# Layer one's first matrix in groups 4 to 7 by seven half-block products instead of eight, for two of the three token blocks

## The chip, the core and the metric

The kernel runs on one core of one Trainium2 chip. The metric is the time of one execution on the device, in microseconds.

## The reference

Attention over 2 x 8 heads with a window and block sums, then two feed-forward layers. The change touches layer one (`_moe_ref`):

```python
# x: 1536 tokens x 512, from the attention
h = x @ w_in                                  # 512 x 2048
x = (h * (1.0 / (1.0 + np.exp(-1.702 * h)))) @ w_out    # 2048 x 512
gate = 1.0 / (1.0 + np.exp(-(x @ w_gate)))    # layer two, 512 x 1536 each
out = (gate * (x @ w_val)) @ w_out2           # 1536 x 512
```

## The kernel before

The tokens are three blocks of 512 (`blk` 0 to 2), held transposed: 128 partitions x 4 chunks of 128 channels x 512 tokens. Every number that TensorE multiplies is split into a high and a low half (`xH`, `xL`; of a weight H and L), and a product of two is three matmuls: low x high, high x low, high x high. A group `g` is 256 columns of the first matrix and the same 256 rows of the second; layer one has 8 groups, layer two 6.

`first` (L368) makes the two 128-column halves of `x @ w_in` for one group and one block: 2 x 12 matmuls of 128x128 by 512 into PSUM banks `ps_h` (`project`, L352), then for each the sigmoid on ScalarE and `gate_by` (L358): the product with the sigmoid on VectorE, its high half (`gh`) on ScalarE, its low half (`gl`) on GpSimd. `second` (L395) multiplies `gh` and `gl` with the second matrix in four m-steps of 6 matmuls (`ps_o`), each added into the SBUF tile `acc` on VectorE (L429). `mm3` (L344) issues the matmuls of both.

Layer two does blocks 0 and 1 of its first matrices in another way, `pair` (L262). A group's two column halves and the two channel halves (LO, HI) make a 2x2 matrix of half blocks, blocks 0 and 1 by channel halves another, and seven products ("1" to "7") of half blocks or of sums of them stand for the eight plain ones. The sums of the weights come from `combine` (L200): high and low half are added again (L205), four sums are built (L214) and split (L219, L220). The sums of the inputs come from `token_sums` (L239). Products share banks x, v and y: product 1 is copied from x into y, 2 adds into x, 6 and 7 and then 4 add into y, 3 into v behind 5; `keep` (L285) copies a bank to SBUF and `total` (L289) adds it to another. Block 2 goes the plain way by half products, `single` (L323).

Weights come as 64-bit words, by 1 MB DMAs on SP's queue (`fetch`, L157), two at a time. `decode` (L91) makes H and L of a matrix with four VectorE instructions of 128x1024 (L102, L105, L107, L112) and two on ScalarE; it is a generator of five parts, and `pull` draws one part between the pieces of the main work. H and L lie in rings of 8, 4 and 2 tiles (`w_slots`, `w_a`, `w_b`, `w_c`), 14 in all; a group's load starts at a fixed step of the main loop.

Groups 0 and 1, blocks 0 and 1, run between the attention's units. Behind the attention (from L746) the steps are (g, blk), each a `first` with the `second` of the step before. `first` has 2 PSUM banks (`ps_h`) and `second` 6 (`ps_o`); in layer two it is the other way round.

The order of SP's instructions is the written one. That of every other engine is chosen when the program is built, by a planner that plays it through with durations of its own: of the instructions that are ready it takes the one written first. `keep_in_program_order` ties an instruction behind the one that was written before it on its engine, in issue order alone. An instruction that writes a tile waits for the last reader of what lay in its place.

Of the kernel before, what the change touches and what calls it, by code (L numbers as in the profile page):

```python
# [28 lines left out]
def attention_moe_moe2_kernel(ctx: ExitStack, tc: tile.TileContext, ins: dict, out: bass.AP):  # L29
# [34 lines left out]
    class Slots:  # L64


        def __init__(self, tag):
            self.tag, self.order, self.i = tag, [], 0

# [14 lines left out]
    w_slots, sg_slots, gh_slots, gl_slots = (Slots(t) for t in ("w", "sg", "gh", "gl"))  # L84
    w_a = pool([w_slots], 8, "w_a")
# [5 lines left out]
    def decode(raw, hi_out, lo_out):  # L91
# [8 lines left out]
        ts = nc.vector.tensor_scalar  # L100

        ts(out=af, in0=head.bitcast(F32), scalar1=F64_MAX, scalar2=-F64_MAX, op0=ALU.min, op1=ALU.max)  # L102
        nc.scalar.activation(af, af, AF.Prelu, scale=REBIAS, alpha=-2.0 ** 32)  # L103
        yield
        ts(out=b, in0=tail, scalar1=29, scalar2=None, op0=ALU.logical_shift_right)  # L105
        yield
# [3 lines left out]
        nc.scalar.copy(hi_out, af)  # L110
        yield
        nc.vector.tensor_tensor(out=lo_out, in0=af, in1=hi_out, op=ALU.subtract)  # L112
        yield
# [18 lines left out]
    groups = [(1, g) for g in range(n1)] + [(2, g) for g in range(n2)]  # L132
    steps = [(1, g, blk) for blk in range(NTB) for g in range(2)]
    steps += [(1, g, blk) for g in range(2, n1 - 2) for blk in range(NTB)]
    steps += [(1, g, blk) for g in (n1 - 2, n1 - 1) for blk in range(2)] + [(1, g, 2) for g in (n1 - 2, n1 - 1)]
# [11 lines left out]
    pieces, weights, raws, ready = [], {}, [], {}  # L147
# [20 lines left out]
    def load(slots, layer, g, i):  # L168
        raw, shape = raws.pop(0)
        hi, lo = (slots.tile(list(shape), F32R, name=f"w{layer}_{g}_{i}{x}") for x in "HL")  # L170
        parts = decode(raw, hi.rearrange("p a n -> p (a n)"), lo.rearrange("p a n -> p (a n)"))
        for step, _ in enumerate(parts):
            if step == 1 and (layer, g) != (1, 0):
                fetch()
            yield
        return hi, lo

    def load_group(layer, g):
        tiles = weights[layer, g] = []
        ready[layer, g] = 0  # L180
        for i in range(len(mats[layer])):
            tiles += yield from load(w_slots, layer, g, i)
            ready[layer, g] += 1
            yield

    class Ring:


        def __init__(self, pool):
            self.pool = pool  # L190

        def tile(self, shape, dtype, name):
            return self.pool.tile(shape, dtype, tag="w", name=name)

# [5 lines left out]
    def combine(g, i):  # L200

        hi, lo = weights[2, g, i]
        flat = "p a n -> p (a n)"
        w, s = (wtmp.tile([P, KC, GF * P], F32, tag=t, name=f"{n}{g}_{i}") for t, n in (("da", "wf"), ("db", "ws")))
        nc.vector.tensor_tensor(out=w.rearrange(flat), in0=hi.rearrange(flat), in1=lo.rearrange(flat), op=ALU.add)  # L205
        yield
        s = s.rearrange("p a (k f) -> p a k f", f=P)
        for n, a, b, op in (
            (0, block(w, 1, 0), block(w, 1, 1), ALU.add),
            (1, s[:, 0], block(w, 0, 0), ALU.subtract),  # L210
            (2, block(w, 0, 0), block(w, 1, 0), ALU.subtract),
            (3, block(w, 0, 1), s[:, 1], ALU.subtract),
        ):
            nc.vector.tensor_tensor(out=s[:, n], in0=a, in1=b, op=op)  # L214
            if n % 2:
                yield
        sh, sl = (Ring(w_b).tile([P, 4, KC // 2, P], F32R, name=f"s{x}{g}_{i}") for x in "HL")
        flat = "p a k f -> p (a k f)"
        nc.scalar.copy(sh.rearrange(flat), s.rearrange(flat))  # L219
        nc.vector.tensor_tensor(out=sl.rearrange(flat), in0=s.rearrange(flat), in1=sh.rearrange(flat), op=ALU.subtract)  # L220
        sums[g, i] = sh, sl
        yield

    sums = {}

    def prepare():

        for g in range(-1, n2):
            for n in ([0, 1] if g < 0 else [0, 2, 1]):
                to = g + (n != 2)  # L230
                if to < n2:
                    weights[2, to, n] = yield from load(Ring(w_c if n == 2 else w_a), 2, to, n)
                    ready[2, to, n] = 1
                    yield
            for n in range(2 * (g + 1 < n2)):
                yield from combine(g + 1, n)
                ready[2, g + 1, "s", n] = 1

    def token_sums():  # L239
# [3 lines left out]
        for name, x, y, to in (  # L243
# [6 lines left out]
            if name == "4":  # L250
                h, l = xH[1][:, LO], xL[1][:, LO]
            else:
                h, l = (tp.tile([P, KC // 2, TB], F32R, tag=f"t{name}{x}", name=f"t{name}{x}") for x in "HL")
# [8 lines left out]
    def pair(g):  # L262


        def sums_of(n, i):
            return tuple(x[:, n] for x in sums[g, i])

        def a(i, r, c):
            return tuple(block(x, r, c) for x in weights[2, g, i])
# [11 lines left out]
        def new(b, i):  # L281
            ps[b, i] = ps_f.tile([P, TB], F32, tag="o", name=f"ps_{b}")
# [10 lines left out]
        def out(i, to, x, own=None):  # L293
            if i:
# [5 lines left out]
        for n in "1256734":  # L300
            for i in range(2):
# [21 lines left out]
    def single(g):  # L323

        for f in range(GF):
            sg = None
            for i in range(2):
                wh, wl = weights[2, g, i]
                ps = ps_f.tile([P, TB], F32, tag="o", name="ps_h" if i == 0 else "ps_v")
# [5 lines left out]
                if i == 0:  # L335
                    sg = sg_slots.tile([P, TB], F32, "sg")
                    nc.scalar.activation(sg, ps, AF.Sigmoid)
                else:
                    gate_by((2, g, 2, f), ps, sg)
# [12 lines left out]
    def project(wh, wl, f, blk, name):  # L352
        ps = ps_h.tile([P, TB], F32, tag="h", name=name)
# [14 lines left out]
    def first(layer, g, blk, batch=False):  # L368
        w = weights[layer, g]
# [25 lines left out]
    def second(layer, g, blk, last, lag=False):  # L395
        wh, wl = weights[layer, g][-2:] if layer == 1 else weights[2, g, 2]
# [7 lines left out]
        for m in range(4):  # L404
            ps = ps_o.tile([P, 512], F32, tag=o_tag, name="ps_o")
# [3 lines left out]
            elif last and blk == NTB - 1 and m == 3:  # L409

                r0 = blk * TB + m * P
                for n0 in range(0, 512, 256):
                    n = slice(n0, n0 + 256)
                    if n0:
                        ps = ps_o.tile([P, 512], F32, tag=o_tag, name="ps_o")
# [24 lines left out]
    ps_o, o_tag = ps_h, "h"  # L440
# [3 lines left out]
    coming = (x for n in range(2) for x in load_group(*groups[n]))  # L444

    def pull(n):
        for _ in range(n):
            if next(coming, True):
                break

    def need(layer, g, n):
        while ready.get((layer, g), 0) < n:
            pull(1)

    with tc.manual_schedule(engines={mybir.EngineType.SP}), ExitStack() as es:
# [236 lines left out]
        def filler():  # L692
            for layer, g, blk in steps[:EARLY]:
                while (blk + 1) * 2 * HP - 1 + LD > now[0]:
                    yield
                need(layer, g, len(mats[layer]) - 1)
                yield from first(layer, g, blk, batch=True)
                need(layer, g, len(mats[layer]))
# [47 lines left out]
    with tc.manual_schedule(engines={mybir.EngineType.SP}):  # L746
        w_b, w_c = pool([w_slots], 4, "w_b"), pool([w_slots], 2, "w_c")
# [4 lines left out]
        ps_o = ctx.enter_context(tc.tile_pool(name="ps_o", bufs=6, space=PSUM, reuse_waits="tile"))  # L752
        o_tag = "o"
        pull(1000)
        coming = load_group(*groups[2])
        pull(1)
        prev, folding = None, iter(())
        for step in steps[EARLY:]:
            layer, g, blk = step
            need(layer, g, len(mats[layer]) - 1)  # L760
            for _ in first(*step):
                pull(1)
                next(folding, None)
            if prev:
                need(*prev[:2], len(mats[prev[0]]))
                for _ in second(*prev, prev[1] == ends[1]):
                    pull(1)
                    next(folding, None)
                if prev == (1, n1 - 1, 1):
                    folding = token_sums()  # L770
            prev = step
            if blk == (NTB - 1 if g < 2 else 0) and (1, g + 1) in groups and (1, g + 1) not in ready:
                pull(1000)
                coming = load_group(1, g + 1)
            elif step == (1, n1 - 1, 0):
                pull(1000)
                coming = prepare()
        ps_f, ps_o, o_tag = ps_o, ps_h, "h"

        def ahead(g):  # L780
            if (2, g, "s", 1) not in ready:
                pull(1)

        for g in range(n2):
            for key in ((2, g, 0), (2, g, 1), (2, g, "s", 0), (2, g, "s", 1)):
                while key not in ready:
                    pull(1)
            for _ in folding:
                pass
            rest = second(*prev, prev[0] == 1)  # L790
            for slot, _ in enumerate(pair(g)):
# [7 lines left out]
            while (2, g, 2) not in ready:  # L799
                pull(1)  # L800
            rest = (x for blk in range(2) for x in second(2, g, blk, g == ends[2]))
# [49 lines left out]
```

## Time and profile before

| | us |
|---|---|
| median of 3 runs | 628.73 |
| lowest, highest | 628.70, 629.77 |
| the profiled execution | 629.99 |
| its span, from the first to the last instruction | 628.1 |
| TensorE, VectorE, ScalarE, GpSimd busy in it | 613.1, 430.8, 282.5, 194.8 |

The granted TensorE clock is 0.997 of full speed over the span. PE is TensorE, DVE is VectorE, ACT is ScalarE, POOL is GpSimd; L349 is line 349. A matmul's record lasts some 390 ns and overlaps the next one's, so TensorE's time is read from the distance between starts. Idle time of an engine that nothing waits for costs nothing.

### The profile page before, as it was taken

To read this page: it belongs to the slowest core of one execution; us is meant where nothing else is said; L and a number is where in the kernel's file an instruction comes from. 1 tells how busy PE (TensorE), PEld (TensorE's weight loads), DVE (VectorE), ACT (ScalarE), POOL (GpSimd) and SP (SyncE) were. 2 spreads that over 40 slices of the span, in tenths; PEclk is the share of its full clock that TensorE was granted. 3 is DMA by queue.
4 is the path that set the end of the run, shared out by engine and by line. 5 is a ranking of instruction groups with operands and counts; after the bars stand their busy time and mean duration, and the time that the engine had idled before them with its cause. 6 is when DMAs were issued, how large, how long until landed. Compare 5 with 4: busy or idle time off the path is not lost.

```text
span 628.1 us, 8342 instructions
## 1 busy us (share of the span) xinstructions
PE 613.1 (98%) x3162; PEld 499.9 (80%) x3162; DVE 430.8 (69%) x628; ACT 282.5 (45%) x560; POOL 194.8 (31%) x164
## 2 busy tenths in 40 slices
PE   7898999999999999999999999999999999999997
PEld 4676787778888888888888887888887888888886
DVE  6699666488976665565379995279499479496524
ACT  4688657546443334232246645444344244333310
POOL 6797676233132313132222030120031120130210
PEclk9899999999999999999999999999999999999999
DMA  9997752044521222100001304012113012100004
GB/s 311 347 328 254 242 126 64 2 134 141 176 86 67 68 67 68 67 2 1 0 13 61 129 0 135 0 68 78 57 67 118 17 67 74 61 1 0 2 33 168
DMA packets 25160, 58.08 MB, mean 92 GB/s; under 512 B 1568, under 2 KB 1824, under 8 KB 25120
## 3 DMA queue, kind: packets, MB, share of 16 engines
q1 hardware_dynamic: 24400, 56.24, 27.6%
q10 hardware_dynamic: 720, 1.31, 0.6%
q8 instruction: 25, 0.41, 0.3%
q14 instruction: 15, 0.12, 0.1%
HBM read 53.08 MB, written 3.15 MB: 90 GB/s over the span
## 4 chain that ended last, share of the span: by engine, by line
PE 86%; DVE 9%; ACT 2%; issue 1%; DMA 1%; SPq 0%; DVEq 0%; ACTq 0%
PE ps_o L349 35%; PE ps_h L349 20%; PE ps_v L124 8%; PE ps_y L124 7%; PE ps_x L124 5%; PE ps_h L124 4%; PE ps_s L559 3%; PE ps_x L611 2%; PE ps_p L592 1%; DVE wf L205 1%; DVE ws L214 1%; DMA vt<-in_vt 1%; ACT e L572 1%; DVE nm L564 1%; DVE sg L364 1%
## 5 line engine op out<-in xcount | busy, mean ns | idle before, releaser
L366 POOL TENSOR_TENSOR gl<-sg,gh 128x512 fp32r<-128x512 f32 x84 | 119.5, 1424 | 393.7 <-ACT gh L365 372.0
L429 DVE TENSOR_TENSOR acc<-ps_o,acc 128x512 f32<-128x512 f32 x143 | 97.2, 686 | 56.9 <-PE ps_o L349 56.8
L365 ACT CAST gh<-sg 128x512 fp32r<-128x512 f32 x84 | 52.0, 620 | 89.8 <-DVE sg L364 79.6
L349 PE MATMUL ps_o<-gh,w_1L 128*128 128x512 f32 x192 | 74.5, 395 | 1.6 <-ACT gh L365 1.5
L349 PE MATMUL ps_h<-xH,w_0L 128*128 128x512 f32 x192 | 75.2, 396 | 0.5 <-DVE acc L429 0.5
L349 PE MATMUL ps_o<-gl,w_1H 128*128 128x512 f32 x192 | 75.4, 393 | 0.0
L349 PE MATMUL ps_h<-xL,w_0H 128*128 128x512 f32 x192 | 75.0, 391 | 0.0
L349 PE MATMUL ps_o<-gh,w_1H 128*128 128x512 f32 x192 | 74.8, 390 | 0.0
L349 PE MATMUL ps_h<-xH,w_0H 128*128 128x512 f32 x192 | 74.8, 390 | 0.0
L364 DVE TENSOR_TENSOR sg<-ps_h,sg 128x512 f32<-128x512 f32 x48 | 32.9, 687 | 44.1 <-ACT sg L373 43.8
L349 PE MATMUL ps_o<-w_2H,gl 128*128 128x512 f32 (+1 forms) x146 | 56.2, 388 | 1.0 <-ACT acc L425 0.6
L349 PE MATMUL ps_o<-w_2H,gh 128*128 128x512 f32 (+1 forms) x146 | 56.4, 386 | 0.0
L349 PE MATMUL ps_o<-w_2L,gh 128*128 128x512 f32 (+1 forms) x146 | 56.4, 386 | 0.0
L373 ACT ACTIVATE sg<-ps_h 128x512 f32<-128x512 f32 x48 | 28.3, 595 | 61.2 <-PE ps_h L349 61.2
L107 DVE SCALAR_TENSOR_TENSOR da<-da,db 128x1024 uint32<-128x1024 uint32 x34 | 43.9, 1290 | 14.4 <-ACT da L103 14.0
L103 ACT ACTIVATE da<-da 128x1024 f32<-128x1024 f32 x34 | 36.1, 1061 | 30.6 <-DVE da L102 28.6
L349 PEld LDWEIGHTS ps_o<-gh,w_1L 128*128 128x128 f32 x192 | 35.9, 188 | 9.3 <-ACT gh L365 2.0
L349 PEld LDWEIGHTS ps_h<-xH,w_0L 128*128 128x128 f32 x192 | 36.0, 188 | 8.2 <-DVE acc L429 0.9
L349 PEld LDWEIGHTS ps_h<-xH,w_0H 128*128 128x128 f32 x192 | 36.0, 188 | 7.6
L349 PEld LDWEIGHTS ps_o<-gh,w_1H 128*128 128x128 f32 x192 | 36.1, 188 | 7.3
L349 PEld LDWEIGHTS ps_o<-gl,w_1H 128*128 128x128 f32 x192 | 36.1, 188 | 7.3 <-POOL gl L366 0.2
L349 PEld LDWEIGHTS ps_h<-xL,w_0H 128*128 128x128 f32 x192 | 36.0, 188 | 7.4
(162 smaller groups left out, 1244.5 us busy)
## 6 DMA issues: line engine op xcount, KB each, us to landing
raw<-in_moe_w_out SPq DMA_DIRECT2D x13, 1024.0 KB, 4.9
raw<-in_moe_w_in SPq DMA_DIRECT2D x8, 1024.0 KB, 7.3
raw<-in_moe_w_gate SPq DMA_DIRECT2D x6, 1024.0 KB, 5.1
raw<-in_moe_w_val SPq DMA_DIRECT2D x6, 1024.0 KB, 5.1
q<-in_q SPq DMA_DIRECT2D x20, 256.0 KB, 7.5
vwin<-in_v SPq DMA_DIRECT2D x6, 768.0 KB, 8.1
k<-in_k SPq DMA_DIRECT2D x8, 400.0 KB, 6.5
out<-acc SPq DMA_DIRECT2D x11, 256.0 KB, 2.0
```

What stands on the lines that cost most here:

```text
L103: nc.scalar.activation(af, af, AF.Prelu, scale=REBIAS, alpha=-2.0 ** 32)
L107: nc.vector.scalar_tensor_tensor(out=a, in0=a, scalar=3, in1=b, op0=ALU.logical_shift_left, op1=ALU.bitwise_or)
L124: nc.tensor.matmul(ps, lhsT=a[x][:, kk, :], rhs=b[y][:, kk, :], start=start and i == 0, stop=i == n - 1, skip_group_check=True,)
L205: nc.vector.tensor_tensor(out=w.rearrange(flat), in0=hi.rearrange(flat), in1=lo.rearrange(flat), op=ALU.add)
L349: nc.tensor.matmul(ps, lhsT=a, rhs=b, start=i == 0, stop=i == n - 1)
L364: nc.vector.tensor_tensor(out=sg, in0=val, in1=sg, op=ALU.mult)
L365: nc.scalar.copy(gh, sg)
L366: nc.gpsimd.tensor_tensor(out=gl, in0=sg, in1=gh, op=ALU.subtract)
L373: nc.scalar.activation(sg, ps, AF.Sigmoid, scale=1.702 if layer == 1 else 1.0)
L429: nc.vector.tensor_tensor(out=a[:, m, :], in0=ps, in1=a[:, m, :], op=ALU.add)
L559: nc.tensor.matmul(ps[:, j, :], lhsT=t[:, j, :], rhs=kt[:, j, :], start=False, stop=j == G - 1)
L611: nc.tensor.matmul(ps[64 * e:64 * e + 64, j, :], lhsT=x[:, h * D:(h + 1) * D], rhs=y[:, j, 64 * e:64 * e + 64], start=n == 0, stop=n == le ...
```

## The change

- In groups 4 to 7 of layer one, blocks 0 and 1 of the first matrix go through `pair(1, g)`, block 2 through `single(1, g)`. Both now take the layer; layer one has one first matrix, the order "1526374", and each finished piece gets its own sigmoid and gate.
- `input_sums` makes the sums of the attention's output in 13 parts: eight parts behind step (2, 0), the rest behind step (3, 1). Its adds on VectorE are kept in program order, the low halves are GpSimd's. Sum "4" overwrites the low channel half of block 1.
- `load` joins `decode` and `combine`, for both layers: the sums are built from the decoded float before it is split, so the add of high and low halves (L205) is gone.
- The rings of weight tiles become 14 named places, 8 and 6: `take` gives the oldest free one, `drop` frees a matrix behind its last use, and the loads run on through all matrices in one order, whenever two tiles are free.
- PSUM behind the attention: 4 banks for the first steps, 4 for the second steps; in layer two 6 and 2 as before.
- The second steps of groups 4 to 7 run inside the pairs and singles, block 1 before block 0. `pair(1, 7)` runs straight behind `pair(1, 6)`; `single(1, 6)` follows it.

The core of the diff:

```diff
+    def take(shape, name, key):
+        p, tag = w_free.pop(0)
+        w_held.setdefault(key, []).append((p, tag))
+        return p.tile(shape, F32R, tag=tag, name=name)
+    def drop(*key):
+        w_free.extend(w_held.pop(key))
...
+    def load(layer, g, i, early):
+        while len(w_free) < 2:
+            yield
...
+        nc.vector.tensor_tensor(out=lo.rearrange(flat), in0=af, in1=hi.rearrange(flat), op=ALU.subtract)
+        weights[layer, g, i] = hi, lo
+        yield
+        if layer == 1 and (g < PAIRED or i == 1) or layer == 2 and i == 2:
+            yield
+            return
+        w = af.rearrange("p (a n) -> p a n", n=shape[2])
+        s = wtmp.tile([P, 4, KC // 2, P], F32, tag="db", name=f"ws{layer}_{g}_{i}")
...
-        nc.vector.tensor_tensor(out=w.rearrange(flat), in0=hi.rearrange(flat), in1=lo.rearrange(flat), op=ALU.add)
...
+        tt(out=f3, in0=f2, in1=f3, op=ALU.subtract)
+        nc.scalar.copy(h3, f3)
...
+        nc.gpsimd.tensor_tensor(out=l3, in0=f3, in1=h3, op=ALU.subtract)
...
+            if layer == 1:
+                gate = sg_slots.tile([P, TB], F32, "sg")
+                nc.scalar.activation(gate, x, AF.Sigmoid, scale=1.702)
+                gate_by((1, g, *to), x, gate)
+                return
...
-        for n in "1256734":
-            for i in range(2):
+        for n in ("1526374", "1256734")[layer - 1]:
+            for i in range(layer):
...
-        w_b, w_c = pool([w_slots], 4, "w_b"), pool([w_slots], 2, "w_c")
+        places(6, "w_b")
...
-        ps_o = ctx.enter_context(tc.tile_pool(name="ps_o", bufs=6, space=PSUM, reuse_waits="tile"))
+            for x, n in (("a", 4), ("b", 2))
+        ps_f, ps_s = Slots("h", (ps_a, 4)), Slots("h", (ps_h, 2), (ps_b, 2))
...
+            if step == (1, 2, 0):
+                folding = itertools.islice(sums_1, 8)
+            elif step == (1, PAIRED - 1, 1):
+                for _ in folding:
+                    pass
+                folding = sums_1
...
+        for g in range(PAIRED, n1):
+            need((1, g, 0), (1, g, 0, "s"))
...
+            if g < top:
+                run(pair(1, g), second(1, g - 1, 2, False), (0, 2, 4, 5))
+                drop(1, g - 1, 1)
+            else:
+                run(pair(1, g), seconds(1, g - 1, 1, 0), range(7))
+            drop(1, g, 0, "s")
+            need((1, g, 1))
+            if g != top - 1:
+                n = min(g, top - 1)
+                run(single(1, n), seconds(1, g, 1, 0), (0, 0, 1, 1, 2, 2, 3, 3))
+                drop(1, n, 0)
```

## Rows read from the trace of the kernel before

**Rows 1.** The page's first part: busy us, share of the span, instructions.
```profile
PE 613.1 (98%) x3162; PEld 499.9 (80%) x3162; DVE 430.8 (69%) x628; ACT 282.5 (45%) x560; POOL 194.8 (31%) x164
```
**Rows 2.** The chain of waits in order of time: start, length, what, how many.
```profile
253.10 5.44 PE ps_h L349 x24
258.54 5.44 PE ps_o L349 x24
```
**Rows 3.** What TensorE waited for behind the attention: total us, times, longest.
```profile
PE ps_o L349 <- ACT acc L425: 0.6, 1, 0.6
...
PE ps_h L349 <- DVE acc L429: 0.5, 1, 0.5
...
PE ps_o L349 <- DVE acc L429: 0.3, 1, 0.3
```
**Rows 4.** Busy us by stretch: PE, PEld, DVE, ACT, POOL; granted clock, DMA share, GB/s.
```profile
140.00:340.00 200.00, 200.00 (x884) 165.64 (x884) 134.68 (x176) 76.75 (x111) 52.83 (x37) 1.00 0.20 64
340.00:380.00 40.00, 39.58 (x175) 32.46 (x173) 39.17 (x51) 23.17 (x33) 8.53 (x6) 1.00 0.20 62
```
**Rows 5.** Groups of instructions, shapes apart: count, busy us, mean ns; idle before, releaser.
```profile
L366 POOL TENSOR_TENSOR gl<-sg,gh 128x512 fp32r<-128x512 f32 x84 | 119.5, 1424 | 393.7 <-ACT gh L365 372.0 <-PE ps_o L349 11.2 <-issue 9.8
...
L429 DVE TENSOR_TENSOR acc<-ps_o,acc 128x512 f32<-128x512 f32 x143 | 97.2, 686 | 56.9 <-PE ps_o L349 56.8
...
L365 ACT CAST gh<-sg 128x512 fp32r<-128x512 f32 x84 | 52.0, 620 | 89.8 <-DVE sg L364 79.6 <-PE ps_o L349 6.5 <-DVE ws L214 2.9
...
L107 DVE SCALAR_TENSOR_TENSOR da<-da,db 128x1024 uint32<-128x1024 uint32 x34 | 43.9, 1290 | 14.4 <-ACT da L103 14.0
...
L364 DVE TENSOR_TENSOR sg<-ps_h,sg 128x512 f32<-128x512 f32 x48 | 32.9, 687 | 44.1 <-ACT sg L373 43.8
...
L102 DVE TENSOR_SCALAR da<-raw 128x1024 f32<-128x1024 f32 x33 | 28.6, 866 | 0.4
...
L105 DVE TENSOR_SCALAR db<-raw 128x1024 uint32<-128x1024 uint32 x33 | 28.3, 859 | 0.9 <-DMA raw<-in_moe_w_out 0.6
...
L373 ACT ACTIVATE sg<-ps_h 128x512 f32<-128x512 f32 x48 | 28.3, 595 | 61.2 <-PE ps_h L349 61.2
...
L112 DVE TENSOR_TENSOR w_0L<-da,w_0H 128x1024 fp32r<-128x1024 f32 x14 | 18.5, 1325 | 1.5 <-ACT w_0H L110 1.5
...
L220 DVE TENSOR_TENSOR sL<-ws,sH 128x1024 fp32r<-128x1024 f32 x12 | 14.6, 1216 | 2.0 <-ACT sH L219 2.0
...
L214 DVE TENSOR_TENSOR ws<-wf 128x256 f32<-128x256 f32 x24 | 10.5, 479 | 0.2
...
L205 DVE TENSOR_TENSOR wf<-w_0H,w_0L 128x1024 f32<-128x1024 f32 x6 | 9.2, 1541 | 0.1
...
L287 ACT COPY sg<-ps_v 128x512 f32<-128x512 f32 x12 | 7.0, 587 | 16.3 <-PE ps_v L124 16.3
...
L214 DVE TENSOR_TENSOR ws<-wf,ws 128x256 f32<-128x256 f32 x12 | 7.0, 584 | 0.2
...
L214 DVE TENSOR_TENSOR ws<-ws,wf 128x256 f32<-128x256 f32 x12 | 5.0, 414 | 0.0
```
**Rows 6.** Instructions in order of time, 361 and 468 us: start, length, engine, operation.
```profile
361.18 1.22 DVE L205 TENSOR_TENSOR wf<-w_0H,w_0L 128x1024 f32<-128x1024 f32 x1
...
467.98 1.30 POOL L366 TENSOR_TENSOR gl<-sg,gh 128x512 fp32r<-128x512 f32 x1 [1.95 <-ACT gh L365]
...
468.07 2.29 DVE L205 TENSOR_TENSOR wf<-w_1H,w_1L 128x1024 f32<-128x1024 f32 x1
```
**Rows 7.** TensorE in order of time, at its three waits (in brackets: idle before, releaser).
```profile
127.64 0.50 PE L349 MATMUL ps_h<-xH,w_0L 128*128 128x512 f32 x1 [0.48 <-DVE acc L429]
...
380.21 0.50 PE L349 MATMUL ps_o<-w_2H,gl 128*128 128x512 f32 x1 [0.64 <-ACT acc L425]
...
473.28 0.50 PE L349 MATMUL ps_o<-w_2H,gl 128*128 128x512 f32 x1 [0.28 <-DVE acc L429]
```

More of the change, by code (lines that the diff above doesn't have):

```diff
@@ L100, in decode @@
         ts = nc.vector.tensor_scalar
+        hi, lo = (take(list(shape), f"w{layer}_{g}_{i}{x}", (layer, g, i)) for x in "HL")
+        flat = "p a n -> p (a n)"
         ts(out=af, in0=head.bitcast(F32), scalar1=F64_MAX, scalar2=-F64_MAX, op0=ALU.min, op1=ALU.max)
@@ L109, in decode @@
         )
-        nc.scalar.copy(hi_out, af)
+        nc.scalar.copy(hi.rearrange(flat), af)
         yield
-        nc.vector.tensor_tensor(out=lo_out, in0=af, in1=hi_out, op=ALU.subtract)
+        nc.vector.tensor_tensor(out=lo.rearrange(flat), in0=af, in1=hi.rearrange(flat), op=ALU.subtract)
[6 more added lines that the diff above has]
+        s = wtmp.tile([P, 4, KC // 2, P], F32, tag="db", name=f"ws{layer}_{g}_{i}")
+        for n, x, y, op in (
+            (0, block(w, 1, 0), block(w, 1, 1), ALU.add),
+            (1, s[:, 0], block(w, 0, 0), ALU.subtract),
+            (2, block(w, 0, 0), block(w, 1, 0), ALU.subtract),
+            (3, block(w, 0, 1), s[:, 1], ALU.subtract),
+        ):
+            nc.vector.tensor_tensor(out=s[:, n], in0=x, in1=y, op=op)
+            if n == 1:
+                yield
+        while len(w_free) < 2:
+            yield
+        sh, sl = (take([P, 4, KC // 2, P], f"s{layer}_{g}_{i}{x}", (layer, g, i, "s")) for x in "HL")
+        flat = "p a k f -> p (a k f)"
+        nc.scalar.copy(sh.rearrange(flat), s.rearrange(flat))
+        yield
+        nc.vector.tensor_tensor(out=sl.rearrange(flat), in0=s.rearrange(flat), in1=sh.rearrange(flat), op=ALU.subtract)
+        weights[layer, g, i, "s"] = sh, sl
         yield
@@ L131, in attention_moe_moe2_kernel @@
     n2 = w_gate.shape[1] // (GF * P)
[L132 to L135, printed above, removed]
+    steps = [(1, g, blk) for blk in range(2) for g in range(2)]
     ends = {1: n1 - 1, 2: n2 - 1}
@@ L166, in fetch @@
             raws.append((raw, (P, n, m // 2)))
[L168 to L184, printed above, removed]
@@ L224, in attention_moe_moe2_kernel, with t_tile @@
[L224 to L237, printed above, removed]
+    def t_tile(name):
+        return tp.tile([P, KC // 2, TB], F32R, tag=f"t{name}", name=f"t{name}")
@@ L260, in attention_moe_moe2_kernel, with pair @@
     tsum = {}
-    def pair(g):
+    def pair(layer, g):
         def sums_of(n, i):
-            return tuple(x[:, n] for x in sums[g, i])
+            return tuple(x[:, n] for x in weights[layer, g, i, "s"])
         def a(i, r, c):
-            return tuple(block(x, r, c) for x in weights[2, g, i])
+            return tuple(block(x, r, c) for x in weights[layer, g, i])
         b11, b21, b22 = ((xH[n][:, h], xL[n][:, h]) for n, h in ((0, LO), (0, HI), (1, HI)))
@@ L321, in pair, with single @@
                 yield
-    def single(g):
+    def single(layer, g):
         for f in range(GF):
             sg = None
-            for i in range(2):
-                wh, wl = weights[2, g, i]
-                ps = ps_f.tile([P, TB], F32, tag="o", name="ps_h" if i == 0 else "ps_v")
+            for i in range(layer):
+                wh, wl = weights[layer, g, i]
+                ps = ps_f.tile([P, TB], F32, name="ps_h" if i == 0 else "ps_v")
                 for j in range(2):
@@ L368, in first @@
     def first(layer, g, blk, batch=False):
[L369 removed]
+        w = weights[layer, g, 0]
         def sigmoid(layer, ps):
@@ L443, in attention_moe_moe2_kernel, with need @@
     EARLY_UNITS = 10
-    coming = (x for n in range(2) for x in load_group(*groups[n]))
+    order = [(1, g, i) for g in range(n1) for i in range(2)] + [(2, 0, 0), (2, 0, 1)]
+    for g in range(n2):
+        order += [(2, h, i) for h, i in ((g + 1, 0), (g, 2), (g + 1, 1)) if h < n2]
+    coming = (x for n, key in enumerate(order) for x in load(*key, n < 2))
     def pull(n):
         for _ in range(n):
[L448 to L453, printed above, removed]
+            next(coming, None)
+    def need(*keys):
+        for key in keys:
+            tries = 0
+            while key not in weights:
+                pull(1)
+                tries += 1
+                assert tries < 100, (key, w_free, w_held)
     with tc.manual_schedule(engines={mybir.EngineType.SP}), ExitStack() as es:
@@ L751, in attention_moe_moe2_kernel @@
         tp = ctx.enter_context(tc.tile_pool(name="tp", bufs=1, reuse_waits="tile"))
-        ps_o = ctx.enter_context(tc.tile_pool(name="ps_o", bufs=6, space=PSUM, reuse_waits="tile"))
[L753 to L761, printed above, removed]
+        ps_a, ps_b = (
+            ctx.enter_context(tc.tile_pool(name=f"ps_{x}", bufs=n, space=PSUM, reuse_waits="tile"))
+            for x, n in (("a", 4), ("b", 2))
+        )
@@ L762, in attention_moe_moe2_kernel, with run @@
+        ps_f, ps_s = Slots("h", (ps_a, 4)), Slots("h", (ps_h, 2), (ps_b, 2))
+        folding, sums_1 = iter(()), input_sums()
+        def run(main, rest=iter(()), after=()):
+            for n, _ in enumerate(main):
                 pull(1)
                 next(folding, None)
-            if prev:
[L765 to L770, printed above, removed]
@@ L771, in attention_moe_moe2_kernel @@
-            prev = step
[L772 to L778, printed above, removed]
+                for _ in range(after.count(n)):
+                    next(rest, None)
+            for _ in rest:
+                pull(1)
+                next(folding, None)
@@ new lines, in seconds @@
+        def seconds(layer, g, *blks):
+            for blk in blks:
+                yield from second(layer, g, blk, g == ends[layer])
+        steps = [(1, g, 2) for g in range(2)] + [(1, g, blk) for g in range(2, PAIRED) for blk in range(NTB)]
+        prev = None
+        for step in steps:
+            need((*step[:2], 0))
+            run(first(*step))
+            if step[2] == 2:
+                drop(*step[:2], 0)
+            if prev:
+                need((*prev[:2], 1))
+                run(second(*prev, False))
+                if prev[2] == 2:
+                    drop(*prev[:2], 1)
+            if step == (1, 2, 0):
[4 more added lines that the diff above has]
+                folding = sums_1
+            prev = step
@@ L780, in ahead @@
+        folding = token_sums()
+        run(single(1, top), second(1, top - 1, 2, False), range(4))
+        drop(1, top, 0)
+        drop(1, top - 1, 1)
+        prev = (1, top)
+        ps_f, ps_s = Slots("h", (ps_a, 4), (ps_b, 2)), Slots("h", (ps_h, 2))
         def ahead(g):
-            if (2, g, "s", 1) not in ready:
+            if (2, g, 1, "s") not in weights:
                 pull(1)
         for g in range(n2):
-            for key in ((2, g, 0), (2, g, 1), (2, g, "s", 0), (2, g, "s", 1)):
-                while key not in ready:
-                    pull(1)
+            need((2, g, 0), (2, g, 1), (2, g, 0, "s"), (2, g, 1, "s"))
@@ L798, in attention_moe_moe2_kernel @@
                 pass
-            while (2, g, 2) not in ready:
-                pull(1)
-            rest = (x for blk in range(2) for x in second(2, g, blk, g == ends[2]))
-            for _ in single(g):
+            drop(*prev, prev[0])
+            drop(2, g, 0, "s")
+            drop(2, g, 1, "s")
+            need((2, g, 2))
+            rest = seconds(2, g, 0, 1)
+            for _ in single(2, g):
                 ahead(g + 1)
```

114 lines of the change are left out of this document (69 added, 45 removed).

## Prediction

> **What bounds the kernel now.** I read four views, from coarse to fine. The page's busy times come first [rows 1]: TensorE is busy for 98% of the span, VectorE (DVE) for 69%. A busy TensorE proves little, since the records of its products overlap, so the second view is the chain of waits in order of time, in the middle of layer one [rows 2]: 24 products of a first step in 5.44 us, then 24 of a second step in 5.44 us, with nothing between them. That is 0.2267 us a product, and it is the price that I use. The third view, what TensorE waited for [rows 3], shows how little else there is: three waits behind the attention stage, 0.6, 0.5 and 0.3 us, each for an accumulator eviction. The fourth, busy times by stretch [rows 4], says who would be next: from 140 to 340 us TensorE is busy all 200 us, while DVE works 134.7 of them (67%); from 340 to 380 us DVE works 39.2 of 40 and TensorE loses 0.4. So behind the attention the number of products sets the time, as long as DVE keeps up. The change takes products away and gives DVE work, so these two are weighed.
>
> **The products.** A group's first matrix takes two blocks x two column halves x 12 = 48 products for token blocks 0 and 1 now; seven half-block products of 6 are 42. Block 2 keeps its 24, the second matrix its 72. Six fewer in each of four groups are 24, and 24 x 0.2267 = 5.44 us, all on the path. **-5.44.**
>
> **What DVE gets.** All durations are of [rows 5]. The sums of one first matrix are two adds of 0.479, one of 0.584, one of 0.414 and the low half, 1.216: 3.17 us, for four groups 12.7. Two totals a group, of a gate's shape and so at 0.687: 5.5. The input sums are eight DVE instructions of 128x1024; their nearest row is the add of two such tiles in layer two, mean 1.54, so 12.3. (ScalarE's extra copies of about 0.59 us stand beside an engine that is busy 76.8 of the 200 us [rows 4], so I cost them at nothing.) Layer two's first two matrices also come earlier, because a load now goes on as soon as a place is free: 0.866 + 0.859 + 1.290 + 1.325 = 4.34 us each, and 3.17 for their sums, of which I put about 10 us inside this stretch. Together 134.7 + 12.7 + 5.5 + 12.3 + 10 = 175 us in 200 - 5 = 195: DVE goes from 67% to 90%. Taken away, in layer two, are the twelve adds of high and low halves (six at 1.54, six more of the other matrix): 18 us that DVE no longer has there.
>
> **Where DVE falls behind.** The average hides one place. Six of the input sums' DVE instructions are issued within the step of group 2, block 1: 6 x 1.54 = 9.2 us. The step's own work is four evictions (0.686) and two gates (0.687), 4.1; the loading that is drawn along is six of a matrix's five parts, 5.2. That makes 18.5 us of DVE work in a step of 48 products, 10.9 us: DVE ends 7.6 us behind. The later steps of groups 2 and 3 hold 9.3 to 12 us each for 10.9, so it stays behind until group 4, where the 14 places are full, loading stops and a pair's 66 products take 15 us with some 7 us of DVE work. What hides 7.6 us: the second steps get four PSUM banks, each written once in 10.9 us, so an eviction may come 10.88 - 1.36 - 0.69 = 8.8 us late; and between a first step's end and its own second step stand 48 products, 10.9 us, for a chain of 0.595 (sigmoid) + 0.687 (gate) + 0.620 (high half) + 1.424 (low half, POOL) = 3.3, which leaves 7.5. I have no duration for a POOL subtraction of 128x1024; twice the 128x512 row is an estimate of 2.85 us, and two of them ahead of a low half would take 5.7 us of these 7.5. Bounds: 0 (the cover just holds) and 6 (it holds for one of the two); nearer to the stretch of [rows 4] in which DVE was 98% busy and TensorE lost 0.4 in 40 us: **+1.0** for the 70 us of groups 2 and 3.
>
> Beside POOL, DVE is not its own master. The add of two 128x1024 tiles took 1.22 us at 361.18, and 2.29 us at 468.07, where a POOL subtraction of 1.30 us had started 0.09 us before it [rows 6]: waiting for its end (1.21) and then 1.22 would be 2.43, sharing evenly less. The Trainium skill, SBUF — State Buffer, section Who interferes with whom, says that a DVE instruction with two SBUF inputs contends with a GpSimd instruction that reads SBUF, and that the port is an exclusive lock: the later one waits for the whole of the other. The trace is within 0.14 us of that. By the rule the four new POOL subtractions would stop DVE for up to 11.4 us more in groups 2 and 3; without it nothing is added to the sum above. This is the mechanism of the first rival.
>
> **Within a pair of groups 4 to 7.** Product 4 adds into the bank that product 7 has just left, so DVE's total of 7 (0.687) must be over first. One m-step of six products, 1.36 us, stands between them. If DVE has just begun a decode instruction of 1.325, the total ends 2.01 us after product 7 and TensorE waits 0.65; four times 2.6. The other end is 0, when the queue is empty or more of the second step's products stand there. Group 4's DVE has slack, groups 5 to 7 less: **+0.8**. The other hand-overs have more cover: product 7 after 6 needs ScalarE's copy of 0.587 and has 2.7 us, product 3 after 5 the same copy and more.
>
> **PSUM banks.** The three waits stand at 127.6, 380.2 and 473.3 us [rows 7]. The first is for a bank that first and second steps shared; the first steps now have four of their own, which the attention left before. **-0.5**, bounds 0 and -0.5; what is late next is the eviction of a second step, with four banks instead of six, and each used once in 10.9 us. The other two (0.6 and 0.3) are layer two's, where the second steps still have two banks; DVE has 18 us less to do there, ScalarE the same: **-0.4**, bounds 0 and -0.9.
>
> **Moved, and costed at nothing.** Loads run further ahead, and each draws its DMA with it, on SP's queue: the DMA engines are at 0.20 [rows 4], so the landing is hidden; if it were not, one decode would be late by a transfer, and the group needs it a group later. A matrix that takes a used place has its high-half copy wait on ScalarE for the last product that reads the old one; behind it stand sigmoids and high halves, with 7.5 us of cover. Layer two's second matrix gets its place only when group 7's sums are done; 120 products (27 us) are left for 4.34 + 3.17 us of DVE work. Four high halves of group 7 are written while four of group 6 are unread, in a ring of five: the second of them waits for group 6's last second step, and 24 products of a single block (5.4 us) stand between that and the first reader; without them it would cost 0.62 + 1.42 = 2.0. Holding the input sums in issue order keeps them from moving up into idle DVE time, and costs no more than the backlog above.
>
> **Sum.** -5.44 + 1.0 + 0.8 - 0.5 - 0.4 = -4.5 us. The profiled execution took 629.99 us (span 628.1 and 1.9 around it), and becomes 625.5; it is 1.26 us above the median of the runs, 628.73, so the forecast is **624.2 us**. Its own range is 621.7 to 626.5.
>
> **Rivals.** (a) DVE's backlog decides, and the kernel gets slower. Place: the second steps of group 2, blocks 1 and 2, and again of group 3. Price: 7.6 us behind and 5.7 us of POOL subtractions ahead of the low halves are 13.3 against a cover of 7.5, a stall of 5.8; the second half of the sums, which DVE reaches without having caught up, adds up to 5.7. It decides from 5.44 us of stall on. With half of the second stall: 628.73 - 5.44 + 5.8 + 2.8 = 631.9 us. For it: the doubled add of [rows 6]. Against: PSUM has room for a whole further step, which TensorE can take first, and 40 us of a full DVE cost 0.4 us. 0.09. (b) The pairs give half of it back: all four wait 0.65, and groups 2 and 3 cost 1.0, with none of today's waits gone: 628.73 - 5.44 + 2.6 + 1.0 = 626.9. For it: 1.36 us of cover against queues with instructions of 1.3 us. 0.14. (c) Nothing new waits, and today's three waits go: 628.73 - 5.44 - 1.4 = 621.9. For it: layer one stands at 67% of DVE without any wait. 0.14. (d) The change doesn't do what it says: layer one becomes DVE's. 175 us of work with each two-input instruction held up now and then fills the 200 us that the stretch takes today, and TensorE idles for what it saved: 628.7. For it: 90% leaves 20 us. Against: most of these instructions read PSUM or one tile. 0.06. The forecast holds 0.57.
>
> What can be told from no change here is about 0.2%, 1.26 us: faster is below 627.5, slower above 630.0. The forecast, (b) and (c) are faster, less a little at the edge of (b): 0.83. (d) and that edge are the same: 0.08. (a) is slower: 0.09. The range from 621.2 to 628.4 takes in (b) and (c) and leaves out (a), most of (d) and a little below.
>
> **What would show it.** Right: about 24 fewer matmuls in the trace; in the chain of the groups 4 to 7 pieces of 0.2267 us a product with gaps of a few tenths at most; DVE near 90% from 140 to 335 us with TensorE still at its pitch; layer two starting about 5 us earlier; no add of halves in layer two. Wrong: TensorE waiting in groups 2 and 3 for a low half or an eviction, by microseconds (a); a wait of ps_y products for DVE's total in each pair (b); DVE without idle time through all of layer one (d); or a new wait at the head of layer two for its sums.

## The result and the profile after

The changed kernel takes 623.12 us (622.79 to 623.41, 4 runs) against 629.25 for the kernel before (the median of its three runs above and one more, 630.00, taken together with the changed kernel): 6.1 us less. The ratio on record is 0.9891, with a 95% interval of 0.987 to 0.9913; it is what the quotient to that fourth run gives, where the two medians give 0.990. In another job the ratio was 0.9904 (0.989 to 0.9917). The forecast was 624.2 us. Its profiled execution took 623.11 us, with a span of 621.3.

First the answers to [rows 1, 3, 4]: the page's first part, the busy times of the same two stretches, and all that TensorE waited for from 120 to 622 us.

```profile
PE 605.5 (97%) x3138; PEld 493.4 (79%) x3138; DVE 446.5 (72%) x652; ACT 297.0 (48%) x580; POOL 207.7 (33%) x168
```
```profile
140.00:340.00 200.00, 199.54 (x879) 164.61 (x879) 167.38 (x215) 92.86 (x135) 66.61 (x41) 1.00 0.19 64
340.00:380.00 40.00, 40.00 (x178) 33.07 (x177) 39.62 (x48) 22.48 (x34) 9.57 (x6) 1.00 0.23 79
```
```profile
PE ps_o L384 <- POOL gl L401: 0.4, 1, 0.4
```

24 matmuls fewer (3162 to 3138). VectorE works 167 of the 200 us (84%), TensorE still all but 0.5. The waits of [rows 3] are gone, one has come. At its place, in order of time, other lines left out:

```profile
176.81 0.61 ACT L400 CAST gh<-sg 128x512 fp32r<-128x512 f32 x1
176.98 2.41 POOL L264 TENSOR_TENSOR t2L<-f,t2H 128x1024 fp32r<-128x1024 f32 x1 [3.39 <-ACT t2H L260]
178.28 0.60 ACT L400 CAST gh<-sg 128x512 fp32r<-128x512 f32 x1
179.34 3.72 POOL L401 TENSOR_TENSOR gl<-sg,gh 128x512 fp32r<-128x512 f32 x2
...
181.69 0.50 PE L384 MATMUL ps_o<-gl,w_1H 128*128 128x512 f32 x1
...
183.12 0.51 PE L384 MATMUL ps_o<-gl,w_1H 128*128 128x512 f32 x1 [0.45 <-POOL gl L401]
```

Two gates' low halves (L401) stand on GpSimd behind the input sums' `t2L`, and TensorE waits for each of them. A wait's row is not its whole cost. I take the distance between the starts of successive products and sum what exceeds 0.2267 us, from the attention's last product (near 124 us) on; I call it the excess. Here it is 0.17 + 0.11 at the first low half and 0.62 + 0.12 at the second, where the row has 0.45: a product right behind a wait takes 0.50 us instead of 0.39, and the one after it starts 0.11 late.

With the excess the two profiles close. Before 2.5 us, after 1.2; the products are 24 x 0.2267 = 5.4 less, and the attention ends 0.1 earlier: 5.4 + 1.3 + 0.1 = 6.8 us, which is 628.1 - 621.3.

### The profile page after: what moved, and what is told of

It reads as the page before. It is cut to its first block, busy times and chain, and to the rows that moved or that the text cites. A ratio compares the mean times of both kernels' runs of the same rounds, so it can differ in the third digit from the quotient of the medians.

```text
span 621.3 us, 8331 instructions
## 1 busy us (share of the span) xinstructions
PE 605.5 (97%) x3138; PEld 493.4 (79%) x3138; DVE 446.5 (72%) x652; ACT 297.0 (48%) x580; POOL 207.7 (33%) x168
## 4 chain that ended last, share of the span: by engine, by line
PE 81%; DMA 8%; DVE 5%; POOL 3%; issue 2%; ACT 1%; SPq 0%; POOLq 0%; ACTq 0%
PE ps_o L384 33%; PE ps_v L173 12%; PE ps_y L173 11%; PE ps_h L173 9%; PE ps_x L173 7%; PE ps_h L384 5%; DMA xH<-in_moe_w_out 3%; DMA k<-in_k 3%; DMA vt<-in_vt 2%; PE ps_s L600 2%; POOL gl L401 1%; PE ps_x L652 1%; PE ps_p L633 1%; DVE da L132 1%; DVE w_0L L137 1%
## 5 line engine op out<-in xcount | busy, mean ns | idle before, releaser
L401 POOL TENSOR_TENSOR gl<-sg,gh 128x512 fp32r<-128x512 f32 x84 | 121.9, 1455 | 364.6 <-ACT gh L400 309.6
L384 PE MATMUL ps_o<-gh,w_1L 128*128 128x512 f32 x192 | 72.1, 396 | 1.5 <-ACT gh L400 1.4
L589 POOL TENSOR_SCALAR kx<-k 128x384 f32<-128x384 f32 x24 | 32.4, 1351 | 20.2 <-DMA k<-in_k 11.2
L613 ACT ACTIVATE e<-ps_s,nm 128x128 f32<-128x128 f32 x96 | 34.3, 381 | 9.3 <-DVE nm L605 8.2
L384 PE MATMUL ps_h<-xL,w_0H 128*128 128x512 f32 x96 | 37.6, 392 | 0.4 <-DVE xL L673 0.4
L384 PE MATMUL ps_h<-xH,w_0L 128*128 128x512 f32 x96 | 37.7, 401 | 0.0
L384 PE MATMUL ps_h<-xH,w_0H 128*128 128x512 f32 x96 | 37.4, 390 | 0.0
L384 PEld LDWEIGHTS ps_o<-w_2H,gl 128*128 128x128 f32 x146 | 27.4, 188 | 6.1 <-DVE acc L464 0.3
L399 DVE TENSOR_TENSOR sg<-ps_h,sg 128x512 f32<-128x512 f32 x32 | 21.8, 684 | 14.3 <-ACT sg L408 12.2
L384 PEld LDWEIGHTS ps_o<-w_2H,gh 128*128 128x128 f32 x146 | 27.4, 188 | 5.6
```

The lines of the kernel that those rows point to most:

```text
L384: nc.tensor.matmul(ps, lhsT=a, rhs=b, start=i == 0, stop=i == n - 1)
L399: nc.vector.tensor_tensor(out=sg, in0=val, in1=sg, op=ALU.mult)
L401: nc.gpsimd.tensor_tensor(out=gl, in0=sg, in1=gh, op=ALU.subtract)
L589: nc.gpsimd.tensor_scalar(out=to, in0=x, scalar1=scale, scalar2=None, op0=ALU.mult)
L613: nc.scalar.activation(e[:, j, :], s[:, j, :], AF.Exp, bias=nm[:, j:j + 1], accum_out=sm[:, j:j + 1])
```

## The experiments

The ratios are to the kernel before in the same job (its medians were 629.9 us); the excess is the profiled execution's.

| run | us | of before (95%) | excess, us |
|---|---|---|---|
| e1_plain_products | 627.33 | 0.9956 (0.9944 to 0.9968) | 0.2 |
| e2_banks_alone | 627.51 | 0.9956 (0.9944 to 0.9968) | 0.1 |
| e3_halves_added | 625.73 | 0.9931 (0.9918 to 0.9945) | 3.2 |
| e4_low_on_vector | 627.28 | 0.9950 (0.9933 to 0.9967) | 5.2 |
| e5_sums_free | 633.74 | 1.0070 (1.0057 to 1.0083) | 9.6 |
| e6_five_pairs | 631.04 | 1.0019 (1.0011 to 1.0028) | 10.8 |
| e7_cover_taken | 626.00 | 0.9950 (0.9937 to 0.9964) | 3.4 |
| e8_sums_earlier | 625.06 | 0.9931 (0.9919 to 0.9943) | 2.4 |
| e9_one_low_half | 623.69 | 0.9899 (0.9886 to 0.9913) | 1.2 |
| e10_low_and_one | 622.84 | 0.9888 (0.9874 to 0.9901) | 0.4 |
| e11_five_and_low | 623.75 | 0.9904 (0.9890 to 0.9917) | 3.1 |
| e12_changed_again | 623.41 | 0.9904 (0.9890 to 0.9917) | 1.2 |

**What carries the gain: e1, e2, e3.** e1 is the changed kernel with plain steps in all eight groups:

```diff
-    PAIRED = 4
+    PAIRED = 8
+        steps += [(1, g, blk) for g in (top - 1, top) for blk in range(2)] + [(1, g, 2) for g in (top - 1, top)]
-        for g in range(PAIRED, n1):
...
```

> Layer one's groups 4 to 7 by plain products again; loads, places, banks and layer two as in the changed kernel. Theory A (the 24 products carry the gain): 5.44 us come back, the late low half behind the input sums (1.0 us by the distance of starts) goes: 623.1 + 5.44 - 1.0 = 627.5 us, 0.9975 of before; layer two without waits. Rival B (the loads, places and banks carry it, the products are eaten up by new work): 624.5 us or less.

627.33 us; theory A. Its ratio of 0.9975 is missed, though, since the kernel before took 629.9 us in this job and not the 628.7 of its first runs. From e1 to the changed kernel 0.9956 becomes 0.9891 (0.9904 in e12), 3.3 to 4.1 us, and the spans differ by 4.1 (625.4 and 621.3): 5.4 for the products, less 1.0 for the new wait and 0.4 by which the changed kernel's attention ends later. No wait stands in layer two, nor anywhere behind the attention.

e2 is the kernel before with the new PSUM split alone:

```diff
-        ps_o = ctx.enter_context(tc.tile_pool(name="ps_o", bufs=6, space=PSUM, reuse_waits="tile"))
+        ps_f, ps_s = Slots("h", (ps_a, 4)), Slots("h", (ps_h, 2), (ps_b, 2))
```

> The kernel before with the changed PSUM split alone (4 banks for first steps, 4 for second steps behind the attention). Theory A: the wait at 127.6 us goes, which by the distance of starts costs 0.65 + 0.11 us: 0.9988 of before; the two waits in layer two stay. Rival B: the wait is for VectorE's eviction all the same and stays in another place: 1.000.

A gain of 2.8 us by the ratio, 2.4 between the medians, where I expected 0.8. The bank wait went, as forecast, and so did both waits of layer two, whose code is the same. So everything but the products (loads, places, the adds left out, the banks) is worth no more than the banks alone. VectorE is as full there as before; the stretches 360 to 380 and 460 to 480 us, first of the kernel before, then of e2 (the first figure behind the stretch's length is TensorE's, the third DVE's):

```profile
360.00:380.00 20.00, 19.58 (x87) 15.89 (x85) 19.76 (x27) 9.74 (x14) 5.46 (x4) 1.00 0.08 18
...
460.00:480.00 20.00, 19.72 (x88) 16.00 (x87) 19.06 (x24) 7.78 (x12) 6.73 (x5) 1.00 0.10 31
```
```profile
360.00:380.00 20.00, 20.00 (x90) 16.57 (x89) 19.73 (x26) 10.16 (x16) 5.47 (x4) 1.00 0.13 41
...
460.00:480.00 20.00, 20.00 (x90) 16.57 (x89) 18.18 (x25) 8.55 (x12) 4.07 (x3) 1.00 0.19 66
```

e3 puts the adds of high and low halves back into layer two:

```diff
+        if layer == 2:
+            w = wtmp.tile(list(shape), F32, tag="da", name=f"wf{g}_{i}")
+            nc.vector.tensor_tensor(out=w.rearrange(flat), in0=hi.rearrange(flat), in1=lo.rearrange(flat), op=ALU.add)
```

> The changed kernel with the add of high and low halves put back in layer two (twelve VectorE instructions, 18 us). Theory A (these adds made layer two's two waits): waits of 0.3 to 0.6 us come back in layer two, 1.46 us by the distance of starts, 624.0 to 624.6 us. Rival B (they went because the first sums are ready earlier and places are taken from one list): TensorE still waits for nothing there, 623.1 us.

The time is 2.6 us above the changed kernel, more than A gives it, and for another reason. At the two old places TensorE waits for nothing, with all twelve adds there. Its new wait of 1.7 us stands at 347.7, for the last low half of layer one, which kept GpSimd busy for 7.3 us:

```profile
340.35 7.27 POOL L405 TENSOR_TENSOR gl<-sg,gh 128x512 fp32r<-128x512 f32 x1 [10.02 <-ACT gh L404]
...
347.68 0.50 PE L388 MATMUL ps_o<-gl,w_1H 128*128 128x512 f32 x1 [1.70 <-POOL gl L405]
```

With the products behind it this wait is 2.0 us; in e3's profile the attention also ends 1.4 us later than in the changed kernel's. So the adds did not make the old waits; that is B's half. What made them is not settled: every rebuilt plan tried here, e2's included, lost them. How much of e2's gain is the banks themselves and how much the new plan is therefore open beyond the first wait's 0.76 us.

**The 7 us subtraction: e7 and e9.** e7 takes the second steps' products from between product 7 and product 4:

```diff
-                run(pair(1, g), second(1, g - 1, 2, False), (0, 2, 4, 5))
+                run(pair(1, g), second(1, g - 1, 2, False), (0, 1, 2, 3))
```

> The m-steps of the second step inside a pair are written behind products 1, 5, 2 and 6 instead of 1, 2, 3 and 7, so that none stands between product 7 and product 4, which adds into the bank that the total of 7 must leave first. Theory A (the planner fills the place with whatever products are ready): no change, 623.1 us. Rival B (the written order was the cover): four hand-overs wait 0.69 us and VectorE's queue, 626 us.

626.00 us is B's figure, but not in B's way. In the pairs TensorE waits for nothing, as A has it. The changed kernel's chain shows how (start, length, what): product 7 of group 4 ends at 225.8 and product 4 follows at 231.0, with 23 others between them that the planner chose, not the six that were written there.

```profile
224.45 1.36 PE ps_y L173 x6
225.81 2.95 PE ps_h L173 x13
228.76 1.36 PE ps_x L173 x6
230.12 0.91 PE ps_o L384 x4
231.02 1.36 PE ps_y L173 x6
```

But e7 waits 2.0 us at 346.4, where e3 did. GpSimd and VectorE of e7 there, and the product that waits, in order of time, other lines left out:

```profile
338.24 1.21 DVE L278 TENSOR_TENSOR acc<-acc,acc 128x1024 f32<-128x1024 f32 x1
338.54 7.78 POOL L401 TENSOR_TENSOR gl<-sg,gh 128x512 fp32r<-128x512 f32 x1 [8.91 <-ACT gh L400]
339.37 1.22 DVE L137 TENSOR_TENSOR w_0L<-da,w_0H 128x1024 fp32r<-128x1024 f32 x1
...
340.51 1.21 DVE L160 TENSOR_TENSOR s_0L<-ws,s_0H 128x1024 fp32r<-128x1024 f32 x1
341.64 1.22 DVE L285 TENSOR_TENSOR t2L<-acc,t2H 128x1024 fp32r<-128x1024 f32 x1
...
342.78 0.68 DVE L125 TENSOR_SCALAR da<-raw 128x1024 f32<-128x1024 f32 x1
343.38 1.22 DVE L285 TENSOR_TENSOR yL<-acc,yH 128x1024 fp32r<-128x1024 f32 x1
...
344.51 0.68 DVE L128 TENSOR_SCALAR db<-raw 128x1024 uint32<-128x1024 uint32 x1
...
346.37 0.50 PE L384 MATMUL ps_o<-gl,w_1H 128*128 128x512 f32 x1 [1.99 <-POOL gl L401]
```

A subtraction that took 1.3 us in [rows 6], where VectorE was the one to wait, starts 0.3 us behind the first of seven VectorE instructions that read nothing but SBUF, each starting as its predecessor ends, and it ends 1.1 us behind the last of them. It ends as far behind the last one in e3, e4 and e6, so nearly all of its work seems to be done there. Two of the seven, at 342.8 and 344.5, read one tile only, in 0.68 us, and it did not get in beside them either. No VectorE instruction is stretched. e9 moves this one low half to VectorE:

```diff
-        nc.gpsimd.tensor_tensor(out=gl, in0=sg, in1=gh, op=ALU.subtract)
+        low = nc.vector if to == (1, n1 - 1, 2, GF - 1) else nc.gpsimd
+        low.tensor_tensor(out=gl, in0=sg, in1=gh, op=ALU.subtract)
```

> The kernel of e7_cover_taken, with one single low half of 128x512, the last of layer one (group 7, block 2, second column half), on VectorE instead of GpSimd. Theory A (GpSimd's subtraction there took 7.8 us because six VectorE instructions with SBUF inputs in a row kept the port; TensorE's 2.15 us are that): the wait at 344 us goes, 2.26 us by the distance of starts: 623.7 us. Rival B (VectorE's full queue makes the gate late, wherever its low half is made): the wait stays within 0.7 us.

623.69 us, and the wait at 346 us is gone; what is left from 121 to 620 us (second fence) is the one at 181 to 183. VectorE gives the low half 0.68 us at 342.3, in the middle of the same queue, so the queue was not what was late: GpSimd was kept out.

```profile
342.29 0.68 DVE L402 TENSOR_TENSOR gl<-sg,gh 128x512 fp32r<-128x512 f32 x1
```
```profile
PE ps_o L384 <- POOL gl L402: 0.5, 1, 0.5
```

**What makes the wait at 181 us: e4, e8, e10.** e4 moves the four low halves of the input sums:

```diff
-        nc.gpsimd.tensor_tensor(out=l3, in0=f3, in1=h3, op=ALU.subtract)
+        nc.vector.tensor_tensor(out=l3, in0=f3, in1=h3, op=ALU.subtract)
...
```

> The changed kernel with the four low halves of the input sums on VectorE instead of GpSimd (4 x 1.2 us more for VectorE, 12 us less for GpSimd). Theory A (a gate's low half is late because GpSimd works on a 128x1024 subtraction ahead of it, and because that holds VectorE's two-input instructions up): the wait at 181 to 183 us goes, 622.1 us; the input sums' adds all take 1.2 us. Rival B (VectorE's backlog makes it late): the wait grows by up to the 2.4 to 4.9 us that VectorE gets, 624 to 627 us.

Both theories miss the time. The wait at 181 to 183 us is gone, with four subtractions more for VectorE (4.8 us; its busy time from 140 to 340 us stays at 166.8, since it is held up less), so GpSimd's long subtractions are the cause there. The lines of the result show how: the first low half has its input at 177.4 us, and GpSimd begins it at 179.34, as `t2L` ends. The adds do not all take 1.2 us, as A has it: the four between sums are at 1.34 on the mean (1.61 in the changed kernel). But from 339 us on the same low half as in e7 takes 7.9 us, TensorE waits 2.9, and then it runs at half its clock. GpSimd's low half, TensorE's wait, and the 3 us behind it (eight products; granted clock 0.50, the lower of the two levels, 1.2 GHz):

```profile
338.79 7.87 POOL L401 TENSOR_TENSOR gl<-sg,gh 128x512 fp32r<-128x512 f32 x1 [10.55 <-ACT gh L400]
```
```profile
PE ps_o L384 <- POOL gl L401: 2.9, 1, 2.9
```
```profile
347.00:350.00 3.00, 3.00 (x8) 2.32 (x9) 1.82 (x2) 0.62 (x1) 0.00 (x0) 0.50 0.92 335
```

e10 is e4 with e9's edit.

> The kernel of e4_low_on_vector (all four low halves of the input sums on VectorE) with that same low half of group 7 on VectorE too. Theory A: of e4's 5.3 us of excess the 5.0 behind 343 us go, half-speed products included, and neither the wait at 181 to 183 us nor another comes: 622.3 us, 0.8 us under the changed kernel in the same job. Rival B (VectorE is too full for them): 625 us or more.

622.84 us, theory A: an excess of 0.4 and no wait behind the attention. It is the fastest of all by its median, 0.6 us under the changed kernel in the same job (623.41); the intervals, 0.9874 to 0.9901 and 0.9890 to 0.9917, overlap, so that it is faster is likely and not shown.

e8 starts the first eight parts of the input sums two steps earlier:

```diff
-            if step == (1, 2, 0):
+            if step == (1, 0, 2):
```

> The changed kernel with the first eight parts of the input sums two steps earlier, still on GpSimd and tied. Theory A (backlog and GpSimd's long subtractions meet in the step of group 2, block 1; the step before has idle VectorE time): the wait at 181 to 183 us goes, 622.1 us. Rival B (GpSimd's subtraction ahead of a gate's low half is enough by itself): the wait moves with the sums, 623.1 us.

Worse than either. The wait at 181 goes, and TensorE waits at 125.4 and at 154.9 us instead:

```profile
PE ps_o L384 <- DVE acc L464: 1.0, 1, 1.0
PE ps_o L384 <- ACT acc L460: 0.6, 1, 0.6
```

The first is for an eviction, and an add of the sums (1.22 us, at 123.5) stands ahead of it on VectorE. The second is for a copy of an accumulator on ScalarE. It stands there behind a high half whose gate VectorE makes late, at 153.0, behind a decode instruction of 2.31 us that a low half on GpSimd held up; GpSimd had come to that low half only behind `t2L`. VectorE's idle time that I meant to use was not there.

**How near the edge is: e5, e6, e11.** e5 lets the planner place the input sums:

```diff
-            tc.keep_in_program_order(nc.vector.tensor_tensor(**x))
+            nc.vector.tensor_tensor(**x)
```

> The changed kernel without the tie of the input sums' adds to their written place. Theory A (the tie costs nothing but that the sums can't move up into idle VectorE time): the planner starts them earlier, the backlog in groups 2 and 3 shrinks, the wait at 181 to 183 us goes, 622.1 us. Rival B (the tie keeps them from getting in the way): they move ahead of gates and evictions and TensorE waits more, 624 us or more.

Rival B, and more: some 10 us over the changed kernel, slower than before. The adds are ready early and are taken before the evictions that TensorE needs; behind the attention TensorE waits

```profile
PE ps_o L384 <- DVE acc L464: 3.3, 1, 3.3
PE ps_o L384 <- ACT gh L400: 0.8, 1, 0.8
PE ps_o L384 <- POOL gl L401: 0.8, 1, 0.8
PE ps_o L384 <- ACT acc L460: 0.3, 1, 0.3
```

which is 5.2 us; the excess is 9.6, because after the first wait and again after 150 us some eight products run at half speed. From 130 to 133 us:

```profile
130.00:133.00 3.00, 3.00 (x8) 2.33 (x8) 3.00 (x5) 1.11 (x2) 0.00 (x0) 0.50 0.00 0
```

e6 (`PAIRED = 3`, e8's edit) and e11 (`PAIRED = 3`, the sums behind step (1, 2), e10's two edits) take one group more by pairs.

> Group 3 by pairs too (five groups), the input sums two steps earlier. Theory A (TensorE's count decides as long as VectorE's backlog stays under its cover): six products fewer, 1.36 us, and VectorE 3.2 + 1.4 us more in a stretch that is full: 621.8 to 623 us. Rival B (VectorE is full in groups 2 and 3, each microsecond more comes out at TensorE): 625 us or more.

> Group 3 by pairs too, the input sums one step earlier than in the changed kernel, their low halves and the last low half of layer one on VectorE. Theory A (with GpSimd's long subtractions gone the sixth and fifth pair's products pay): 1.36 us under e10, 621 us. Rival B (VectorE's work in groups 2 and 3 comes out at TensorE, as in e6): 625 us or more, with waits between 140 and 185 us.

Six products are 1.4 us, and both lose more. e6 waits 2.9, 2.3 and 1.0 us (the last low half of layer one, as in e7; a copy of an accumulator; an eviction). The last two stand where e8 has its waits, so they come in part from the sums' earlier place. e11 is without GpSimd's waits and still waits 2.4 us for two evictions; it is 0.9 us behind e10, A's lower 621 is missed and B's 625 as well. Neither plan makes a fifth pair pay. Both moved the sums too, and e6 has the accident of the low half as well, so what the pair costs by itself is not shown.

> The changed kernel itself, for a comparison on the same chip: 0.989 of before, the wait for a low half at 181 to 183 us and no other behind the attention.

As expected: 0.9904, an excess of 1.2, the one wait at 182 to 183 us.

## Why the prediction was right, term by term

**The products, -5.4:** right; e1 against the changed kernel has them.

**Groups 2 and 3, +1.0:** right in size (1.0 by the distance of starts) and place: a gate's low half behind GpSimd's subtractions of 128x1024. Those took 2.4 to 3.4 us (estimate 2.85), the adds 1.49 and 1.61 on the mean (taken: 1.54). e4 and e10 show that GpSimd's part was the necessary one. The backlog was not as worked out: the six adds that I put into one step of 10.9 us start between 141.0 and 174.6 us, and VectorE is idle again for 1.7 us before 188.7, well ahead of group 4. And 1.0 was a choice between bounds of 0 and 6, so that it fits this well is in part luck. VectorE's work from 140 to 340 us was put at 175 us and is 167.

**The port.** The rule that was weighed against [rows 6] holds in this profile too. VectorE's add at 166.8 and GpSimd's `t1L`, in order of time, other lines left out:

```profile
165.07 1.21 DVE L132 SCALAR_TENSOR_TENSOR da<-da,db 128x1024 uint32<-128x1024 uint32 x1
165.12 3.43 POOL L252 TENSOR_TENSOR t1L<-f,t1H 128x1024 fp32r<-128x1024 f32 x1 [2.85 <-ACT t1H L248]
166.21 0.68 DVE L464 TENSOR_TENSOR acc<-ps_o,acc 128x512 f32<-128x512 f32 x1
...
166.81 2.82 DVE L228 TENSOR_TENSOR f<-f,f 128x1024 f32<-128x1024 f32 x1
```

GpSimd's end at 168.55 plus 1.2 us is 169.75; the add ended at 169.63, while the eviction at 166.2, which reads PSUM, took its usual 0.68. The Trainium skill, SBUF — State Buffer, section Who interferes with whom, has it so: a VectorE instruction with at most one SBUF input, outside the 2-port performance modes, does not contend with GpSimd, and one with two contends with a GpSimd instruction that reads SBUF. The prediction used the lock in one direction only, GpSimd holding VectorE up. The dearer one was the other, VectorE keeping GpSimd out for 7 us, which no part of it foresaw; the changed kernel escapes it.

**The pairs, +0.8:** wrong, nothing came. I costed the written order; the planner had put 5 us of other products there, and e7 shows that the written order is not the cover. This step failed as a mechanism.

**Banks, -0.5:** right and too small. The wait's row has 0.48; with the products behind it the distance of starts has 0.76.

**Layer two's waits, -0.4:** they are worth 1.5 us by the distance of starts, and all of it came. The reason that I gave, 18 us less for VectorE (19.7 by the kernel before's rows, 9.2 and 10.5 for the two matrices), failed too: e2 loses the waits without it, and e3 does with the adds put back. What made them go is open, so that this term came out on the right side is luck.

**The sum:** -4.5 forecast, -6.1 between the medians, -6.8 between the profiles; 0.8 of the difference is the pairs, 1.1 layer two, 0.3 the bank. What came is nearest to rival (c), today's three waits gone, with the one new wait of groups 2 and 3 on top. Rival (a) did not happen here. A loss of its size is real: e5 is some 10 us over the changed kernel by the order of eight adds alone. But its waits stand from 125 to 159 us, ahead of the place that (a) names, and so do e6's first two.

## What to carry to other kernels

Count the products first: where TensorE waits for 1.4 us in 500, fewer of them are worth their pitch, and new work on another engine cost nothing here until something TensorE needed queued behind it. What decided then was order more than load: from 140 to 340 us VectorE stood at 83 to 84% in the changed kernel and in e10, and at 80% in e5, where eight adds in another order cost 10 us. (In the stretch of e5's waits, from 125 to 160 us, it stood at 96%, against 88% in the changed kernel: the order had moved the work there.) Change one part at a time before giving a gain to the part that was meant: some 40% of this one also came with the PSUM split alone and the plan rebuilt around it.

## What the runs showed of the hardware

A GpSimd subtraction of 128x512, 1.46 us on the mean in the changed kernel, took 7.3 to 7.9 us beside an unbroken run of VectorE instructions that read SBUF alone (e3, e4, e6, e7). It isn't always so: in the changed kernel the same low half, begun at 340.1 us in such a run, took 1.80 us, and the VectorE instruction waited instead (2.31):

```profile
340.11 1.80 POOL L401 TENSOR_TENSOR gl<-sg,gh 128x512 fp32r<-128x512 f32 x1 [6.83 <-ACT gh L400]
...
340.68 2.31 DVE L285 TENSOR_TENSOR t3L<-acc,t3H 128x1024 fp32r<-128x1024 f32 x1
```

What decides which of the two gets through is open. And a long wait can cost a second time: behind waits of 2.9 us (e4) and 3.3 us (e5) TensorE's granted clock was 0.50 for some eight products, 0.2 us more for each, while behind e7's 2.0 us it was 1.00. One wait's length does not settle it: in e5 the clock was 0.50 again from 150.7 to 153.7 us, behind two waits of 0.8 us each, 2.2 us apart, and in e6 from 156 to 159 us, behind one of 2.3.
